# Slot input sums kept in SBUF, eight turning PSUM banks and other scheduler keys in an attention and soft-MoE kernel

## Chip, cores and metric

One core of a Trainium2 chip. The metric is the device time of one execution in microseconds (us). All times of instructions are from the profile of one execution and count from the start of its span. TensorE, VectorE, ScalarE, GpSimd and SyncE appear in the profile as PE (with PEld for weight loads), DVE, ACT, POOL and SP. The granted clock is the share of TensorE's full clock that the profile shows for a stretch. The record marks a run slow when it is over 1.5% above the fastest of its kernel; L834 is line 834 of that kernel's source. The changed kernel is nine lines longer, so that L834 of before is L843 after it.

## The reference

```
q, k, v: (8, 8, 576, 64) f32; phi: (512, 32); w1: (8, 512, 1024); w2: (8, 1024, 512)
scores = q k^T / 8 under a mask (heads 0-3: last 32 keys; heads 4-7: last 128, every 4th)
x      = softmax(scores) v, laid out as (4608, 512)
logits = x phi
d      = softmax of logits over the 4608 tokens;  slot_input = d^T x         (32 x 512)
slot_out[e] = relu(slot_input[e] w1[e]) w2[e]     for 8 experts of 4 slots
out    = softmax of logits over the 32 slots, times slot_out                 (4608 x 512)
```

## The kernel before

The program lists its operations with dependencies, an estimated cost each and a key. A list scheduler runs once, when the program is built: it walks through model time, picks for each engine, among the operations that can start soonest, the one with the lowest key, hands out PSUM banks, and so fixes each engine's order. Where TensorE would stand idle in model time, the scheduler may put in fillers, matmuls whose result nobody reads; they are meant to keep TensorE busy, so that its granted clock does not fall.

```
FILL = (125, 148)                 # model time, us, in which fillers may be put
...
# in schedule(): TensorE would stand idle from free["pe"] to t0, so fill the gap
if e == "pe" and fill[0] < t0 and free[e] < fill[1]:
    gap = t0 - max(free[e], fill[0])
    n = min(int((gap - 0.15) / 0.216), 64)      # matmuls of 128x512, 0.216 us each
    if gap > 0.4 and n > 0:
        x = filler(n)                            # matmuls whose result nobody reads
        ...
        place(x, ts, "pe")
...
ps  = A(nc.psum_tensor("ps", [128, 8, 512], F32))
psA = ps[:, 7, :]                                # bank 7: slot sums, held throughout
one = [[i] for i in range(7)]
psum = Pool(7, {1: [[6]] + one[:6], 2: [[0, 1], [2, 3], [4, 5]]})
...
PACE = 13.1                                      # key of work of unit u at offset x:
def due(u, x): return u * PACE + x               # due(u, x); 8 units of attention
...
# slot sums of batch b, all eight batches into one bank
i_ = t.matmul(psA[32*g:32*g+32, 256*ty:256*ty+256], sbt(et)[:, i, :],
              sbt((xb0, xb1)[ty])[:, m, :],
              start=b == 0 and i < 4, stop=b == B - 1, skip_group_check=True)
...
# after the last batch: one copy, then "fold" (f32 matmuls), w1, w2
op("dve", lambda vv: vv.tensor_copy(psA_sb[:], psA), r=[b_acc], w=[b_psA], ...)
...
PARTS = [("p3a",3,0,8), ("p0",0,0,16), ("p1",1,0,16), ("p2",2,0,16), ("p3b",3,8,16)]
# matmuls on the five parts of w2 in this order; the row sums stand after p1;
# p2 and p3b are loaded into TT, which attention has to leave first
```

The softmax here doesn't subtract the row's maximum and nothing guards it: scores larger than these inputs give would overflow.

## Time and profile before

| | before |
|---|---|
| time, median of 4 runs (of the later comparison) | 181.65 us (180.95 to 182.5) |
| fold matmuls begin (L768) | 137.9 us |
| row sums, then p2 and p3b (L849, L834) | 149.9, 151.9 us |
| last load (p3b) has landed | 151.8 us |
| slot outputs so_sb made (L860) | 153.24 us |
| end of span | 178.9 us |

The lines behind this table stand in the prediction. From so_sb on, 25.7 us of output follow, 22.4 us of them the output's own transfer.

In the list of waits, "issue" is time in which the engine waits for nothing that the profile shows (columns: total us, times, longest us).

```profile
PE ps L532 <- issue: 3.7, 4, 1.8
```

### The profile page before, as it was taken

To read this page: it belongs to the slowest core of one execution; us is meant where nothing else is said; L and a number is where in the kernel's file an instruction comes from. 1 tells how busy PE (TensorE), PEld (TensorE's weight loads), DVE (VectorE), ACT (ScalarE), POOL (GpSimd) and SP (SyncE) were. 2 spreads that over 40 slices of the span, in tenths; PEclk is the share of its full clock that TensorE was granted. 3 is DMA by queue.
4 is the path that set the end of the run, shared out by engine and by line. 5 is a ranking of instruction groups with operands and counts; after the bars stand their busy time and mean duration, and the time that the engine had idled before them with its cause. 6 is when DMAs were issued, how large, how long until landed. Compare 5 with 4: busy or idle time off the path is not lost.

```text
span 178.9 us, 5741 instructions
## 1 busy us (share of the span) xinstructions
PE 131.7 (74%) x2602; PEld 99.8 (56%) x2602; DVE 116.6 (65%) x262; ACT 92.1 (52%) x132; POOL 27.8 (16%) x56
## 2 busy tenths in 40 slices
PE   0019768885997977978898879788699999889000
PEld 0019557674775955756886757586565569432000
DVE  6980596994279569668859947969974020799200
ACT  2005957843574886568589557477331100599000
POOL 7960402500400250230020010010200000000000
PEclk9999999999699999999999999999999999999655
DMA  5999899999999999999999999999999993299995
GB/s 77 198 235 224 187 214 210 228 223 198 221 208 212 243 216 194 213 212 214 236 202 211 214 214 218 233 216 209 227 216 209 216 196 68 78 420 439 469 469 235
DMA packets 5015, 40.79 MB, mean 228 GB/s; under 512 B 1408, under 2 KB 1408, under 8 KB 1792
## 3 DMA queue, kind: packets, MB, share of 16 engines
q0 software_dynamic: 3600, 30.94, 82.9%
q1 hardware_dynamic: 1392, 9.50, 12.7%
q8 instruction: 20, 0.33, 0.7%
q14 instruction: 3, 0.02, 0.0%
HBM read 61.93 MB, written 9.44 MB: 399 GB/s over the span
## 4 chain that ended last, share of the span: by engine, by line
PE 44%; DVE 32%; ACT 6%; DMA 5%; issue 5%; POOL 1%; DVEq 0%; POOLq 0%
DVE XB L634 9%; DVE PT L584 9%; PE ps L532 7%; PE ps L678 5%; DVE WD L907 5%; DVE VN L599 5%; DMA stg<-in_v_dram 5%; PE ps L651 4%; PE ps L527 4%; PE ps L594 4%; PE ps L924 3%; ACT PT L576 3%; PE ps L569 3%; PE ps L623 2%; PE ps L787 2%
## 5 line engine op out<-in xcount | busy, mean ns | idle before, releaser
L551 ACT ACTIVATE TT<-ps 128x864 f32<-128x864 f32 x32 | 28.6, 896 | 32.9 <-PE ps L532 24.0
L576 ACT ACTIVATE PT<-ps 128x768 bf16<-128x768 f32 x48 | 36.7, 812 | 8.9 <-PE ps L569 8.8
L532 PE MATMUL ps<-ident,stg 96*64 96x96 bf16 x576 | 18.0, 224 | 18.3 <-DMA stg<-in_v_dram 12.8
L634 DVE TENSOR_TENSOR XB<-ps,RV 96x768 bf16<-96x768 f32 x32 | 30.3, 947 | 0.6
L532 PEld LDWEIGHTS ps<-ident,stg 96*64 96x64 bf16 x576 | 15.7, 123 | 20.0 <-DMA stg<-in_v_dram 12.8
L599 DVE COPY VN<-ps 128x768 bf16<-128x768 bf16 x32 | 17.5, 546 | 8.8 <-PE ps L594 8.6
L663 DVE COPY XT<-ps 128x576 bf16<-128x576 bf16 x19 | 11.4, 598 | 13.3 <-PE ps L651 13.2
L623 PE MATMUL ps<-VN,PT 128*128 128x65 bf16 x384 | 17.6, 194 | 1.9 <-DVE PT L584 0.9
L569 PE MATMUL ps<-TT 64*128 64x96 bf16 x384 | 15.1, 204 | 4.2 <-issue 1.1
L594 PE MATMUL ps<-ident,TT 128*128 128x128 bf16 x192 | 16.1, 221 | 1.6 <-issue 1.0
L623 PEld LDWEIGHTS ps<-VN,PT 128*128 128x128 bf16 x384 | 14.4, 98 | 4.0 <-DVE PT L584 1.3
L651 PE MATMUL ps<-ident,XB 96*128 96x96 bf16 x192 | 13.1, 209 | 4.4 <-DVE XB L634 4.3
L527 PE MATMUL ps<-ident,stg 96*128 96x96 bf16 x288 | 14.9, 206 | 0.1
L569 PEld LDWEIGHTS ps<-TT 64*128 64x128 bf16 x384 | 9.5, 94 | 7.9 <-ACT PT L576 1.4
L594 PEld LDWEIGHTS ps<-ident,TT 128*128 128x128 bf16 x192 | 10.9, 98 | 5.4 <-issue 2.4
L651 PEld LDWEIGHTS ps<-ident,XB 96*128 96x128 bf16 x192 | 9.8, 99 | 7.0 <-DVE XB L634 6.0
L584 DVE TENSOR_TENSOR PT<-PT,mask_d 128x768 bf16<-128x768 bf16 x24 | 12.9, 546 | 0.5 <-ACT PT L576 0.2
L527 PEld LDWEIGHTS ps<-ident,stg 96*128 96x128 bf16 x288 | 13.0, 98 | 0.3 <-ACT PT L576 0.3
L584 DVE TENSOR_TENSOR PT<-PT,mask_p 128x768 bf16<-128x768 bf16 x24 | 12.6, 538 | 0.0
L894 PE MATMUL ps<-so_sb,expT 128*128 128x512 bf16 x35 | 10.4, 397 | 0.7 <-DVE stg L907 0.2
L664 ACT ACTIVATE XT<-ps 128x576 bf16<-128x576 bf16 x13 | 8.4, 650 | 3.8 <-PE ps L651 3.5
L678 PE MATMUL ps<-XT,phi_pad 128*128 128x192 bf16 (+1 forms) x64 | 10.2, 306 | 0.2 <-ACT XT L664 0.2
(83 smaller groups left out, 162.6 us busy)
## 6 DMA issues: line engine op xcount, KB each, us to landing
WD<-in_moe_w_dram POOLq DMA_DIRECT2D x7, 1024.0 KB, 27.5
stg<-in_moe_w_dram POOLq DMA_DIRECT2D x2, 2048.0 KB, 19.1
out_dram<-WD SPq DMA_DIRECT2D x1, 4096.0 KB, 11.9
stg<-in_q_dram POOLq DMA_DIRECT2D x8, 288.0 KB, 14.9
stg<-in_k_dram POOLq DMA_DIRECT2D x8, 288.0 KB, 16.7
stg<-in_v_dram POOLq DMA_DIRECT2D x8, 288.0 KB, 18.7
stg<-in_q_dram POOLq DMA_DIRECT2D x4, 576.0 KB, 17.9
stg<-in_k_dram POOLq DMA_DIRECT2D x4, 576.0 KB, 19.8
```

What stands on the lines that cost most here:

```text
L527: i_ = t.transpose(bankb2(pt, a)[:, 96 * kk:96 * kk + 96], two[:, c, :], ident[0:96, 0:96])
L532: i_ = t.transpose(bankb2(pt, a)[64 * hx:64 * hx + 64, 96 * kk:96 * kk + 96], src[:, hx, c, :], ident[0:96, 0:96])
L551: return ac.activation(d, sv, ACTF.Copy)
L569: i_ = t.matmul(pair(sc)[:, hx, QB * x:QB * x + QB], win(u, 1, h01, blk_, bpar)[64 * hx:64 * hx + 64], win(u, 0, h01, blk_, bpar)[64 * hx: ...
L576: op("act", lambda ac: ac.activation(sbt(pt)[:, 0:768].rearrange("p (x n) -> p x n", x=2), pair(sc)[:, :, 0:384], ACTF.Exp, scale=SCALE), ...
L584: return dv.tensor_tensor(p_, p_, m.unsqueeze(1).to_broadcast([128, 2, 384]), AluOp.mult)
L594: i_ = t.transpose(bankb(pv)[:, 128 * m:128 * m + 128], win(u, 2, h01, m, bpar), ident[:, :])
L599: op("dve", lambda dv: dv.tensor_copy(sbt(vn)[:, :, :, 0:64], bankb(pv)[:, 0:768].rearrange("p (m x d) -> p m x d", m=6, x=2)), r=[pv], w= ...
L623: i_ = t.matmul(pair(po)[:, bk, 65 * po_:65 * po_ + 65], sbt(pts[i])[:, o_:o_ + 128], sbt(vn)[:, m, half, 0:65], start=True, stop=True)
L634: op("dve", lambda dv: dv.tensor_tensor(sbt(xb)[:].rearrange("p m (x h d) -> p h x m d", x=2, h=2)[:, h01], pv()[:, :, :, 0:64], sbt(rv)[: ...
L651: i_ = t.transpose(bankb(px)[:, QB * m:QB * m + QB], sbt(xb)[:, m, 128 * x:128 * x + 128], ident[0:QB, 0:QB])
L678: i_ = t.matmul(o_, phi_pad[:, c].rearrange("p j i -> p (j i)"), rhs, start=c == 0, stop=c == 3)
```

## The change

The intent is a shorter attention part: the slot sums of two batches at a time stay in a bank and are then added up in SBUF, so that all eight banks turn and pairs come from four places; other keys let the units overlap more; fillers start earlier, since attention should end earlier.

```
-FILL = (125, 148)
+FILL = (116, 148)
...
-    psA = ps[:, 7, :]
-    one = [[i] for i in range(7)]
-    psum = Pool(7, {1: [[6]] + one[:6], 2: [[0, 1], [2, 3], [4, 5]]})
+    psum = Pool(8, {1: [[i] for i in (6, 7, 0, 1, 2, 3, 4, 5)],
+                    2: [[0, 1], [2, 3], [4, 5], [6, 7]]})
...
-    PACE = 13.1
+    PACE = 10.87
...   (offsets of the stages changed: T 0.5 to 0.57 per step, S 4.0+1.3i to 5.2+1.13i,
       V 4.5 to 3.6, P 8.5+2.0g to 6.7+2.46g, X 13.0+0.8x to 19.2+0.1x, L 15.5 to 17.4)
-                i_ = t.matmul(psA[...], ..., start=b == 0 and i < 4, stop=b == B - 1, ...)
+                i_ = t.matmul(bank(acc)[...], ...,
+                              start=b % 2 == 0 and i < 4, stop=b % 2 == 1 and i % 6 >= 2, ...)
+        if b == 1:
+            op("dve", lambda dv: dv.tensor_copy(psA_sb[:], bank(acc)), ...)
+        elif b % 2:
+            op("dve", lambda dv: dv.tensor_tensor(psA_sb[:], bank(acc), psA_sb[:], AluOp.add), ...)
-    op("dve", lambda vv: vv.tensor_copy(psA_sb[:], psA), ...)        # once, at the end
```

(Also in the diff: a guard in the scheduler, so that nothing is picked that writes a bank not yet handed out, and two costs of the model, 0.22 to 0.28 us for S and 0.35 to 0.44 us for the slot sums.)

More of the change, by code (lines that the diff above doesn't have):

```diff
@@ L192, in schedule @@
                 got, tal, ok, taken = [], 0.0, True, {}
+                if any(t.phys is None and t not in o.alloc for t in o.touch):
+                    continue
                 for t in o.alloc:
@@ L341, in bass_dilated_sliding_attn__then__soft_moe_slots_kernel @@
     psb = ps[:].rearrange("p a x -> p (a x)").bitcast(BF16).rearrange("p (a x) -> p a x", a=8)
-    psA = ps[:, 7, :]
-    one = [[i] for i in range(7)]
-    psum = Pool(7, {1: [[6]] + one[:6], 2: [[0, 1], [2, 3], [4, 5]]})
+    psum = Pool(8, {1: [[i] for i in (6, 7, 0, 1, 2, 3, 4, 5)], 2: [[0, 1], [2, 3], [4, 5], [6, 7]]})
     def ring(ts):
@@ L378, in bass_dilated_sliding_attn__then__soft_moe_slots_kernel @@
     b_id0, b_id, b_sel, b_fold, b_rowm, b_phist, b_phi = [Buf() for _ in range(7)]
-    b_acc, b_psA, b_csum, b_rcs, b_rtok = [Buf() for _ in range(5)]
+    b_psA, b_csum, b_rcs, b_rtok = [Buf() for _ in range(4)]
     b_expT, b_expX = [Buf() for _ in range(B)], Buf()
@@ L503, in bass_dilated_sliding_attn__then__soft_moe_slots_kernel @@
     U = [dict() for _ in range(NU)]
-    XB, XT, ET = {}, {}, {}
+    XB, XT, ET, ACC = {}, {}, {}, {}
     def win(u, t, h01, i, bpar):
@@ L537, in st_T @@
            mode="h" if ty == 0 else "f",
-           key=due(u, 0.5 * j))
+           key=due(u, 0.57 * j))
         def ev(ac):
@@ L552, in st_T @@
         op("act", ev, r=[pt], **{"w" if j == 0 else "a": [b_TT[u % 2]]}, cost=0.8,
-           key=due(u, 0.8 + 0.5 * j))
+           key=due(u, 0.8 + 0.57 * j))
     def bankb2(t, a):
@@ L573, in pe @@
             return i_
-        k0 = due(u, 4.0 + 1.3 * i)
-        op("pe", pe, r=[b_TT[u % 2]], w=[sc], alloc=[sc, pt], cost=0.22, mode="r", key=k0)
+        k0 = due(u, 5.2 + 1.13 * i)
+        op("pe", pe, r=[b_TT[u % 2]], w=[sc], alloc=[sc, pt], cost=0.28, mode="r", key=k0)
         op("act", lambda ac: ac.activation(
@@ L596, in pe @@
             return i_
-        k0 = due(u, 4.5 + 2.0 * g)
+        k0 = due(u, 3.6 + 2.0 * g)
         op("pe", pe, r=[b_id, b_TT[u % 2]], w=[pv], alloc=[pv, vn], cost=0.35, key=k0)
@@ L626, in pe @@
             return i_
-        k0 = due(u, 8.5 + 2.0 * g)
+        k0 = due(u, 6.7 + 2.46 * g)
         op("pe", pe, r=list(pts.values()) + [vn], w=[po], alloc=al, cost=0.46, key=k0)
@@ L653, in pe @@
             return i_
-        k0 = due(u, 13.0 + 4.0 * bpar + 0.8 * x)
+        k0 = due(u, 19.2 + 4.0 * bpar + 0.1 * x)
         op("pe", pe, r=[b_id, xb], w=[px], alloc=al, cost=0.31, key=k0)
@@ L680, in pe @@
             return i_
-        k0 = due(u, 15.5 + 4.0 * (b % 2))
+        k0 = due(u, 17.4 + 4.0 * (b % 2))
         op("pe", pe, r=[x0, x1, b_phi], w=[lg], alloc=[lg], cost=1.0, key=k0)
@@ L716, in st_L @@
         xb0, xb1 = XB[b, 0], XB[b, 1]
+        if b % 2 == 0:
+            ACC[b // 2] = tile(psum, 1)
+        acc = ACC[b // 2]
         def pe3(t):
@@ L721, in pe3 @@
                 g = (m + 2 * ty) % 4
-                i_ = t.matmul(psA[32 * g:32 * g + 32, 256 * ty:256 * ty + 256],
+                i_ = t.matmul(bank(acc)[32 * g:32 * g + 32, 256 * ty:256 * ty + 256],
                               sbt(et)[:, i, :], sbt((xb0, xb1)[ty])[:, m, :],
-                              start=b == 0 and i < 4, stop=b == B - 1,
+                              start=b % 2 == 0 and i < 4, stop=b % 2 == 1 and i % 6 >= 2,
                               skip_group_check=True)
             return i_
-        op("pe", pe3, r=[et, xb0, xb1], a=[b_acc], cost=0.35, mode="c", key=k0 + 4.0)
+        op("pe", pe3, r=[et, xb0, xb1], after=list(acc.ready), a=[acc],
+           alloc=[acc] if b % 2 == 0 else [], cost=0.44, mode="c", key=k0 + 4.0)
+        if b == 1:
+            op("dve", lambda dv: dv.tensor_copy(psA_sb[:], bank(acc)), r=[acc], w=[b_psA],
+               cost=0.6, key=k0 + 4.6)
+        elif b % 2:
+            op("dve", lambda dv: dv.tensor_tensor(psA_sb[:], bank(acc), psA_sb[:], AluOp.add),
+               r=[acc], w=[b_psA], cost=0.6, key=k0 + 4.6)
     W_AFTER = {2: ["w10"], 3: ["w11"], 4: ["w12"], 5: ["w13"], 6: ["w14"],
@@ L762, in bass_dilated_sliding_attn__then__soft_moe_slots_kernel @@
     op("dve", lambda vv: vv.reciprocal(rcs[:], rcs[:]), w=[b_rcs], cost=0.1, key=K1)
-    op("dve", lambda vv: vv.tensor_copy(psA_sb[:], psA), r=[b_acc], w=[b_psA], cost=0.65, key=K1)
     fo = tile(psum, 1)
```

## The prediction

> **What bounds the kernel now.** I read, in this order, the page's rows and queue table, its chain, a table of windows over the last 60 us, the last loads with the timeline of what uses them, and the waits.
>
> ```profile
> span 178.9 us, 5741 instructions
> ...
> PE 131.7 (74%) x2602; PEld 99.8 (56%) x2602; DVE 116.6 (65%) x262; ACT 92.1 (52%) x132; POOL 27.8 (16%) x56
> ...
> DMA  5999899999999999999999999999999993299995
> ...
> q0 software_dynamic: 3600, 30.94, 82.9%
> ...
> q8 instruction: 20, 0.33, 0.7%
> ...
> PE 44%; DVE 32%; ACT 6%; DMA 5%; issue 5%; POOL 1%; DVEq 0%; POOLq 0%
> ```
>
> The last line, the chain that ended last, calls the kernel bound by compute: 44% TensorE, 32% VectorE, 5% DMA. The change is made with that in view. The DMA row says something else: the 16 engines are busy in nearly every slice until about 147 us, fall to 3 and 2 tenths for two slices, and are then filled by the output. The queue table sizes that wall. The loads' packets (q0) take 82.9% of 16 engines' span: 0.829 x 178.9 = 148.3 us on each engine. Instruction fetches add 0.7%, 1.3 us. The bytes begin to flow at about 2.4 us. So 2.4 + 148.3 + 1.3 = 152.0 us is when the loads end, as long as their number, size and rate stay as they are. The windows show whether anything interrupts them (columns: window and length in us; busy us of PE, PEld, DVE, ACT, POOL with counts; granted clock; DMA share; GB/s).
>
> ```profile
> 118.00:128.00 10.00, 7.33 (x158) 5.71 (x154) 8.54 (x19) 6.55 (x9) 1.58 (x3) 1.00 1.03 221
> 128.00:138.00 10.00, 9.72 (x117) 5.79 (x117) 6.71 (x17) 2.78 (x6) 0.00 (x0) 1.00 1.02 218
> 138.00:148.00 10.00, 10.00 (x130) 6.36 (x133) 1.41 (x3) 0.98 (x2) 0.00 (x0) 1.00 0.95 200
> 148.00:154.00 6.00, 5.62 (x162) 4.96 (x151) 0.87 (x2) 0.47 (x1) 0.00 (x0) 1.00 0.20 41
> 154.00:166.00 12.00, 10.55 (x37) 3.66 (x36) 11.90 (x19) 11.20 (x18) 0.00 (x0) 1.00 0.88 363
> ```
>
> Nothing does: the share is 1.0 up to 138 and 0.95 up to 148, and the windows from 4 to 138 us all move 207 to 221 GB/s (counted as landed bf16). Then: who is late at the end, compute or loads? Two issue rows give the time to landing of the last two parts of the second weight matrix, p2 and p3b; the timeline shows their issue and their use.
>
> ```profile
> TT<-in_moe_w_dram POOLq DMA_DIRECT2D x1, 2048.0 KB, 20.0
> ...
> TT<-in_moe_w_dram POOLq DMA_DIRECT2D x1, 1024.0 KB, 25.1
> ...
> 126.16 1.05 POOL L430 DMA_DIRECT2D TT<-in_moe_w_dram  x2 [5.87 <-PE ps L569]
> ...
> 149.94 2.04 PE L849 MATMUL ps<-rowm,expT 128*128 128x1 bf16 x36
> 151.91 1.21 PEld L834 LDWEIGHTS ps<-TT,hT 128*32 128x32 bf16 x48
> 151.91 1.49 PE L834 MATMUL ps<-TT,hT 128*32 128x256 bf16 x48
> 152.02 0.38 DVE L854 RECIPROCAL rtok<-ps 128x36 f32<-128x36 f32 x1 [4.59 <-PE ps L849]
> 153.24 0.48 DVE L860 TENSOR_SCALAR so_sb<-ps,rcs 128x256 bf16<-128x256 f32 x1 [0.84 <-PE ps L834]
> ```
>
> p2 lands at 126.2 + 20.0 = 146.2 us. p3b, issued half a microsecond after it, lands at 126.7 + 25.1 = 151.8 us, which agrees with the 152.0 above. TensorE comes to these parts at 151.91, after its row sums (L849), and then runs all 48 matmuls: 32 on p2, which has lain there for 5.7 us, and 16 on p3b, which has just come. So compute and loads finish within 0.1 us of each other: two bounds, of which the chain shows one.
>
> [...] The loads read f32 and land bf16, so 214 GB/s landed is 428 GB/s read[...]. [...] Here GpSimd waits for a free buffer before each load, but each load takes 15 to 25 us from issue to landing, so the queue stays full meanwhile. [...] after TensorE stood still from 42.3 to 44.1 us its clock was 0.50 to 0.66 until 48 us. Pauses of 1.1 us (near 77 and 103 us) left it at 1.00. [...] Before, one holds the slot sums throughout, and a pair can take three places.
>
> **The change part by part.**
> Slot sums: the accumulation over eight batches becomes four over two. The matmuls stay the same in number; only their start and stop flags differ. VectorE empties the bank four times in place of once. The one copy of 128x512 f32 took 0.69 us (L763); I take 0.7 us for each add as well. That is 3 x 0.7 = 2.1 us more on VectorE (116.6 to 118.7), spread over some 100 us; only the last stands on the tail, where the copy stood: 0 to 0.1 us.
> Banks: eight singles and four pair places for seven and three. What this can take away is in the waits of TensorE for an engine that empties a bank:
>
> ```profile
> PE ps L532 <- ACT TT L551: 1.0, 2, 0.5
> PE ps L569 <- DVE VN L599: 1.0, 1, 1.0
> PE ps L569 <- ACT PT L576: 0.9, 1, 0.9
> ```
>
> With the smaller ones about 4 us over the whole attention part. Since the order was fixed for seven banks, part of the cost lies in the order itself, so I allow 3 to 8 us in all.
> Keys: a pace of 10.87 for 13.1 and other offsets let a unit start further inside the one before. No instruction is added. The filler matmuls' start moves from 125 to 116, as if the attention's end was expected 9 us earlier. I choose 5 us, for VectorE is already busy 11.2 of 15 us per unit and TensorE 12.5. The fold matmuls (L768), at 137.9 us before, then begin at about 133, and everything up to p1 is done before p2 lands.
> Tail: p2's 32 matmuls can run when it lands at 146.2, and the row sums are done by then too. At 151.8 only p3b's 16 are left. 48 took 1.49 us, of which the last one's latency is 0.27; the step is (1.49 - 0.27) / 47 = 0.026 us. 32 fewer are 0.83 us; the start itself moves from 151.91 to about 151.85. **Sum**: 0.83 + 0.06 = 0.9 us. The output starts 0.9 us earlier and is as long as before, since it is its own DMA wall (363 to 391 GB/s to the end). Of a 5 us gain in compute some 4 us turn into waiting for p3b. If TensorE's clock has fallen by then, the 16 matmuls and the first ones of the output cost about 0.4 us more; at even odds that is 0.2. So 0.7 us off: 181.75 - 0.7 = 181.05, which I round to 181.0, with a profiled span of about 178.2.
>
> **The rivals.**
> A: compute is the only bound, as the chain reads. Then 5 us fewer in attention give 176.8, and the full 9 us give 172.8. Against it stands p3b's landing at 151.8; for it, only if the last loads finish late because they are issued late. The queue speaks against that: p1 was issued at 119.8, p2 at 126.2, and p1 was landing until about 138, so p2 waited in the queue for 10 us and more.
> B: waiting takes the place of compute and lets the clock fall. The fillers end by the scheduler's 148, so TensorE may stand idle for 2 to 4 us before p3b. At half clock the tail loses what the shorter queue won: 181.5 to 182.
> C: VectorE becomes the bound. It carries 2.1 us more, and the new order may make TensorE wait for it. For it: VectorE is 32% of the chain. Even then compute must become slower than before to cost anything, since it now ends level with the loads: 182.5 to 184.
> D: the loads' end itself moves. The last of the 16 engines ends about 4 us after the first (share 0.95, then 0.20, with data until 151), and 20 instruction fetches fall unevenly among them. More fillers mean more instructions. This shifts the end by up to 1 us either way.
>
> **Range and chances.** The DMA wall gives 181.0. The three runs before spread over 181.0 to 182.5, and D gives 1 us either way: 180.0 to 182.2 should hold it 8 times in 10. Faster by over 2% needs 178.1 or less, 3.6 us off, which the loads forbid unless A is right: 0.05. Slower by over 2% needs 185.4, which C alone hardly reaches: 0.02. Within 2%: 0.93.
>
> **What would show it.** Right: the DMA row and the windows' GB/s unchanged up to 147 us; p3b landing at 151 to 152.5; L768 well before 137.9; L834 on TT split in two, 32 soon after 146 and 16 at the end, the latter released by the DMA and with idle time before them; the first so_sb row (L860) at about 152.4 in place of 153.24; four evictions of the slot sums at about 0.7 us each; a chain that now names the load of TT. Wrong: L834 still running without a pause after compute that ends late (C), or the loads landing several us earlier with the share at 1.0 (then the wall was not one, A). A clock under 1.00 around 152 us would show B.

## The result and the profile after

The changed kernel takes 192.75 us (188.91 to 194.32, 4 runs), against 181.65 us. Its fast runs are 1.047 times those of before (95% interval 1.033 to 1.061). All ratios here are the mean time of one kernel's fast runs over that of the other's of the same rounds, so they are not quite the ratios of the medians. Two of the four runs (194.03 and 194.32) are marked slow and are not used in the ratio; medians and ranges are of all runs. The profiled run is a fast one, 191.48 us.

The page of the changed kernel, the lines that answer to those of before:

```profile
span 189.3 us, 5828 instructions
...
DMA  5999999999999999999999999999999300399992
...
q0 software_dynamic: 3600, 30.94, 78.2%
...
q8 instruction: 21, 0.34, 0.7%
...
PE 55%; DVE 14%; ACT 10%; issue 8%; DMA 5%; POOL 1%; DVEq 0%; POOLq 0%
```

The loads are as they were (0.782 x 189.3 = 148.0 us on each engine) and the DMA row is full as long as before. But two slices after it are empty: but for one fetch of instructions, the engines stand still from 151 us until the output begins at 164 us. The page's issue row for p3b and its issue tell that the last load is not what is late: it is issued at 121.5 and lands at 121.5 + 29.7 = 151.2 us.

```profile
TT<-in_moe_w_dram POOLq DMA_DIRECT2D x1, 1024.0 KB, 29.7
...
120.94 1.05 POOL L430 DMA_DIRECT2D TT<-in_moe_w_dram  x2 [4.99 <-PE ps L569]
```

The timeline shows what TensorE does from then on (start, length, engine, line, operation, count):

```profile
149.37 2.04 PE L858 MATMUL ps<-rowm,expT 128*128 128x1 bf16 x36
...
151.48 7.07 PE L933 MATMUL ps<-mask_p,ident 128*128 128x512 bf16 x32
...
158.48 1.06 PE L843 MATMUL ps<-TT,hT 128*32 128x256 bf16 x32
...
159.69 1.67 PE L933 MATMUL ps<-mask_p,ident 128*128 128x512 bf16 x7 [0.16 <-issue]
...
161.30 0.62 PE L843 MATMUL ps<-TT,hT 128*32 128x256 bf16 x16
161.75 0.48 DVE L869 TENSOR_SCALAR so_sb<-ps,rcs 128x256 bf16<-128x256 f32 x1 [9.93 <-PE ps L843]
```

L933 is the filler. 33 fillers stand between the row sums and p2, and 8 between p2 and p3b (the trace lacks two of the records). All data is there at 151.2 us; TensorE then spends 41 x 0.216 = 8.9 us on matmuls that nobody reads. From the first of them to so_sb it is 10.54 us, against 1.33 us from the same point before; so_sb comes 8.51 us later, since that point itself is 0.70 us earlier.

The output is longer too: from so_sb to the end of the span 27.55 us, against 25.66. The packets show where: fifteen of the 16 DMA engines are done at about 186.5 us and one goes on alone until 188.4 (share 0.06). The sum is 8.51 + 1.89 = 10.4 us, the whole difference of the spans.

And attention gained little: the fold begins at 136.7 in place of 137.9 us, 1.2 us, where I had chosen 5. The list of waits of the changed kernel says where the rest is: the same line as before, now with more than twice the time.

```profile
PE ps L532 <- issue: 8.2, 4, 4.3
```

**Where these stalls lie.** I numbered TensorE's records in the trace (weight loads, matmuls and the few waits that stand by themselves) in order of start. Every "issue" stall of more than 0.6 us in the attention part begins at record 193 + 256k (or the next one or two), in both kernels, and some 1.2 to 1.7 us before it ends one instruction fetch of 16 KB (the packets of queue q8) has come in. Some blocks of 256 records, times in us:

```
kernel  record  its block before  its fetch        stall   fetch end
                began                                      to restart
before  1217    37.37             41.54 to 42.63   1.82    1.50
before  1985    58.90             62.75 to 63.72   1.17    1.36
before  3521    97.69             101.48 to 102.65 1.08    1.40
after   1217    34.98             40.09 to 41.03   4.30    1.52
after   2241    64.51             68.30 to 69.19   2.30    1.57
after   3521    95.97             99.91 to 100.88  1.53    1.38
after   5313    150.91            151.25 to 152.17 none    -
```

While the loads keep the DMA engines full (share 0.95 to 1.07 in windows of 6 to 12 us before), the fetch of a block starts some 2 to 5 us after the block before it has begun, mostly 3.7; it takes about 0.95 us, and TensorE goes on 1.2 to 1.7 us after its end. With the usual lag, 256 records so take some 3.7 + 0.95 + 1.4 = 6.1 us (an estimate; the shortest block of a run took 4.8 to 5.9 us). Where TensorE's work is denser, it stalls. The pauses over 0.3 us that begin at a record 193 + 256k add up to 5.7 us before and 12.6 us after. That the fetch is the cause was only read from the trace at this point; the experiments e5 and e6 test it.

The scheduler knows no such stalls. Its own schedule put the fold at 134.9 us before and at 124.1 us after. On the chip it came 3.0 us later than that before, and 12.6 us later after. Fillers for a gap from 138.0 to 145.1 of model time thus ran from 151 to 158 us.

My theory was then: (1) the loads and compute end almost level, as predicted; (2) the late fillers are the loss of 8.5 us; (3) instruction fetches eat most of attention's gain (the granted clock turned out to have a part in this, see e3 and e4), and a 21st fetch that falls into the output costs the other 1.9 us. Rivals: the new order or the added evictions cost the time; or TensorE's clock does.

### The profile page after: what moved, and what is told of

It is laid out like the page before. It is cut to its first block, busy times and chain, and to the rows that moved or that the text cites.

```text
span 189.3 us, 5828 instructions
## 1 busy us (share of the span) xinstructions
PE 141.2 (75%) x2635; PEld 106.6 (56%) x2642; DVE 110.8 (59%) x253; ACT 97.8 (52%) x144; POOL 27.8 (15%) x56
## 4 chain that ended last, share of the span: by engine, by line
PE 55%; DVE 14%; ACT 10%; issue 8%; DMA 5%; POOL 1%; DVEq 0%; POOLq 0%
PE ps L532 10%; PE ps L933 7%; PE ps L527 7%; ACT PT L576 6%; PE ps L623 6%; PE ps L678 5%; DVE WD L916 5%; DMA stg<-in_v_dram 5%; PE ps L594 3%; PE ps L569 3%; PE ps L651 3%; DVE XB L634 2%; PE ps L843 2%; DVE PT L584 2%; PE ps L796 2%
## 5 line engine op out<-in xcount | busy, mean ns | idle before, releaser
L532 PE MATMUL ps<-ident,stg 96*64 96x96 bf16 x576 | 18.3, 234 | 21.0 <-DMA stg<-in_v_dram 12.5
L532 PEld LDWEIGHTS ps<-ident,stg 96*64 96x64 bf16 x576 | 16.9, 131 | 21.9 <-DMA stg<-in_v_dram 12.5
L664 ACT ACTIVATE XT<-ps 128x576 bf16<-128x576 bf16 x25 | 15.7, 656 | 6.7 <-PE ps L651 6.7
L594 PE MATMUL ps<-ident,TT 128*128 128x128 bf16 x192 | 17.0, 226 | 1.1 <-ACT TT L551 1.0
L569 PE MATMUL ps<-TT 64*128 64x96 bf16 x384 | 16.3, 207 | 2.0 <-issue 1.4
L632 DVE RECIPROCAL RV<-ps 96x12 f32<-96x12 f32 x32 | 7.0, 221 | 16.7 <-PE ps L623 16.4
L933 PE MATMUL ps<-mask_p,ident 128*128 128x512 bf16 x59 | 14.5, 382 | 0.8 <-issue 0.7
L594 PEld LDWEIGHTS ps<-ident,TT 128*128 128x128 bf16 x192 | 11.6, 102 | 3.6 <-ACT TT L551 1.5
L584 DVE TENSOR_TENSOR PT<-PT,mask_d 128x768 bf16<-128x768 bf16 x24 | 12.3, 527 | 0.0
L678 PE MATMUL ps<-XT,phi_pad 128*128 128x192 bf16 (+1 forms) x64 | 11.0, 323 | 1.0 <-ACT XT L664 1.0
L651 PEld LDWEIGHTS ps<-ident,XB 96*128 96x128 bf16 x192 | 10.5, 104 | 1.1 <-DVE XB L634 0.4
```

The costliest lines, as they stand in the source:

```text
L532: i_ = t.transpose(bankb2(pt, a)[64 * hx:64 * hx + 64, 96 * kk:96 * kk + 96], src[:, hx, c, :], ident[0:96, 0:96])
L569: i_ = t.matmul(pair(sc)[:, hx, QB * x:QB * x + QB], win(u, 1, h01, blk_, bpar)[64 * hx:64 * hx + 64], win(u, 0, h01, blk_, bpar)[64 * hx: ...
L584: return dv.tensor_tensor(p_, p_, m.unsqueeze(1).to_broadcast([128, 2, 384]), AluOp.mult)
L594: i_ = t.transpose(bankb(pv)[:, 128 * m:128 * m + 128], win(u, 2, h01, m, bpar), ident[:, :])
L651: i_ = t.transpose(bankb(px)[:, QB * m:QB * m + QB], sbt(xb)[:, m, 128 * x:128 * x + 128], ident[0:QB, 0:QB])
L678: i_ = t.matmul(o_, phi_pad[:, c].rearrange("p j i -> p (j i)"), rhs, start=c == 0, stop=c == 3)
```

## The experiments

A table of what the traces show first; "schedule" is where the program's own schedule puts the fold, "stalls" the sum of pauses described above. The times of instructions are of one profiled run each; e5 and e6 ran once, so their state is unknown. Each run is explained below the table; e7 and e9, whose profiled runs were slow, are left out of it.

| run | edit | schedule | fold begins | stalls | so_sb | so_sb to end | time, median us |
|---|---|---|---|---|---|---|---|
| before | | 134.9 | 137.9 | 5.7 | 153.2 | 25.7 | 181.65 |
| after | | 124.1 | 136.7 | 12.6 | 161.75 | 27.55 | 192.75 |
| e1 | after, no late fillers | 124.1 | 135.9 | 11.0 | 152.1 | 25.6 | 180.64 |
| e2 | before, 41 late fillers | 134.9 | 137.2 | 3.9 | 161.6 | 25.6 | 191.98 |
| e3 | banks alone | 131.0 | 135.7 | 6.9 | 152.2 | 25.7 | 180.09 |
| e4 | keys alone | 127.9 | 135.5 | 6.8 | 152.15 | 26.45 | 181.04 |
| e5 | e1, five loads moved back | 124.1 | 134.0 | 7.3 | 163.55 | 26.35 | 192.11 |
| e6 | e1, 128 instructions in front | 124.1 | 136.4 | 10.2 | 152.5 | 27.4 | 182.19 |
| e8 | e3, one load more | 131.05 | 140.8 | 8.5 | 156.8 | 26.0 | 184.60 |
| e10 | e3 again | 131.0 | 139.4 | 7.3 | 154.75 | 25.65 | 183.37 |
| e11 | e3, fillers from 112 | 131.0 | 136.8 | 7.8 | 152.1 | 25.6 | 180.28 |
| e12 | e1, fillers from 106 | 124.1 | 132.5 | 9.6 | 152.15 | 26.55 | 180.66 |

### e1: the changed kernel without late fillers

```
-FILL = (116, 148)
+FILL = (116, 137)
```

> The changed kernel with the window for filler matmuls ended at 137 in place of 148, so that the 33 fillers between the row sums and part p2 of the second weight matrix, and the 8 between p2 and p3b, fall away; nothing else differs. Theory (the late fillers, placed for an attention part that was expected to end at 124 and ends at 136.7, hold TensorE past the landing of the loads): the matmuls on p2 and p3b follow the row sums at about 151.3, so_sb is made at about 152.6 in place of 161.8, the span is 178 to 179 us and the time 180.5 to 182. With 82 TensorE instructions fewer the last instruction fetch no longer falls into the output. Rival 1 (the new order or the extra evictions themselves cost the time): it stays above 186. Rival 2 (TensorE's clock falls without the late fillers): so_sb comes at 152.6 but the clock near 152 is under 1.00 and the time is 182 to 184.

Measured: 180.64 us (179.93 to 180.87), ratio to before 0.997 (0.992 to 1.002). so_sb at 152.08. The loss is gone with one number, and nothing else of the change was touched: the schedule of e1 is that of the changed kernel without the 33 and the 8 fillers. Both rivals fall: neither the order nor the evictions cost time, and the clock did not fall near 152 us: the 48 matmuls on p2 and p3b took 1.71 us with the 0.31 us of waiting for p3b in it, against 1.49 us before at a clock of 1.00. The timeline of e1:

```profile
150.54 1.71 PE L843 MATMUL ps<-TT,hT 128*32 128x256 bf16 x48
151.63 0.34 PEld L843 LDWEIGHTS ps<-TT,hT 128*32 128x32 bf16 x16 [0.31 <-DMA TT<-in_moe_w_dram]
152.08 0.48 DVE L869 TENSOR_SCALAR so_sb<-ps,rcs 128x256 bf16<-128x256 f32 x1 [1.05 <-PE ps L843]
```

The second row is the one the prediction had asked for: 16 weight loads on p3b, released by the DMA of TT after an idle 0.31 us.

### e2: the kernel before with late fillers

```
+        if k_ >= 3:                       # k_ 3: part p2, k_ 4: part p3b
+            late = [op("pe", lf, ..., after=[last_], cost=0.216 * n, ...)]   # n = 33, 8
...
-    last_ = op("pe", pe, ...)
+    last_ = op("pe", pe, ..., after=late)
```

> The kernel before with one thing added: 33 filler matmuls between the row sums and part p2, and 8 between p2 and p3b, as the changed kernel has them. Theory (late fillers): so_sb comes 33 x 0.216 + 8 x 0.216 = 8.9 us later, the time is 189.5 to 193, like the changed kernel. As the TensorE stream passes the same block of 256 instructions at its end, the output should also end 1 to 2 us later than the shift alone. Rival 1 (order or evictions): it stays at 181 to 183, for the fillers would run in time that TensorE waits anyway.

Measured: 191.98 us (189.45 to 193.92; the runs over 193 are marked slow), ratio 1.050 (1.041 to 1.059), about the change's 1.047. so_sb at 161.60. So the same fillers in the old order cost the same. The output did not become longer in the profiled run (25.6 us): the 21st fetch came, but only at 188.4 us, after the output. That part of what I expected missed.

### e3 and e4: the two parts by themselves

e3 takes the change and puts back the old pace, offsets and the old S cost; `FILL = (125, 144)`. e4 takes the kernel before and puts in the new ones; `FILL = (116, 141)`. Neither has late fillers.

> Only the banks part of the change (slot sums in SBUF, eight banks, pairs from four places), with the keys of the kernel before, and the filler window ended at 144 so that no late fillers come. The program's own schedule puts the fold matmuls at 131.0, 3.9 us earlier than before (134.9). Theory (stalls of TensorE at blocks of 256 instructions eat a gain in attention, and the loads set the end): the fold begins at 134 to 138, the time is 180.5 to 182. Rival (the banks help as the schedule says and compute is the bound): the fold begins at 134 and the time falls to 178. Rival (extra evictions on VectorE cost): the fold begins later than 138 and the time is above 183.

Measured: 180.09 us (179.84 to 180.11), ratio 0.994 (0.989 to 1.000). Fold at 135.7, stalls 6.9 us; the time is just under the range that I gave.

> Only the keys part of the change (the pace and the offsets), with seven banks and one accumulator as before, and the filler window 116 to 141 so that no late fillers come. The program's own schedule puts the fold matmuls at 127.9, 7.0 us earlier than before. Theory (stalls at blocks of 256 instructions, loads set the end): the keys pack TensorE's work more densely, so the summed stalls grow from 5.7 us to 9 to 13, the fold begins at 134 to 138, and the time is 180.5 to 182. Rival (compute is the bound): fold near 131, time near 175. Rival (the keys make VectorE the bound): no growth of the stalls, fold later than 138, time above 182.

Measured: 181.04 us (180.88 to 181.18), ratio 1.000 (0.995 to 1.005). Fold at 135.5, in the range; stalls 6.8 us, where I had expected 9 to 13: a miss. In these single traces each part alone has the fold some 2.3 us earlier, and both together (e1) no more: 2.0 us; but e10, which is e3's kernel again, has it 1.5 us later than before, so a gain of this size is within what varies from run to run. The schedules differ by 10.8 us from before to after, the chip's folds by 2.4 at most in these.

Stalls alone do not say how late the fold is against its schedule: e3 and e4 have the same stalls (6.9 and 6.8 us) but are 4.7 and 7.6 us late. What differs is the clock: counted from TensorE's first matmul (12.8 us) to the fold, it was below full for 11 us in e3 and for 22 us in e4. (The time before the first record of the full clock, at 17.0 us before and 18.1 after, counts as below full: the transposes of 96x96 took 281 ns there, as at a clock of 0.50 near 45 us, and 206 ns at 1.00, all in the trace of before.) Over the twelve profiled runs that are not marked slow, lateness is about the stalls (factor 1.0) plus 0.29 us for each us below the full clock, less 5.5 us, to within 0.9 us; this is a fit, not an experiment. By it the 9.6 us that the changed kernel is later than before are some 7 us of stalls (5.7 to 12.6) and some 3 us of clock (8 us to 19 us below full). In e4 TensorE waited for the last load; its mean granted clock was 0.903 (e3: 0.950), and from so_sb to the end it took 26.45 us, close to the 26.55 of e12, where the clock was 0.50 when the load came.

### e5: loads moved, so that the DMA engines pause

```
+    late = [o for o in P.order if o in early_w]          # loads of w10 to w14
+    P.order = [o for o in P.order if o not in early_w]
+    at = P.order.index(last_unit) + 1                    # behind the last unit's load
+    P.order[at:at] = late
```

> As the first run (changed kernel, no late fillers), with the loads of five of the first weight matrices (w10 to w14) moved behind the load of the last attention unit, so that the 16 DMA engines have pauses during the first half of attention; TensorE's order is the same, instruction by instruction. The result stays right; the loads end later, so the time is worse on purpose. Theory (TensorE's stalls come from instruction fetches that queue behind the loads): in the first eight blocks of 256 instructions the fetch starts sooner after its block (lag under 1 us where the engines pause, against 2.5 to 5.1), the stalls up to 76 us fall from 7.7 us to under 3, and the same matmul that began at 70.8 us begins at 63 to 67. Rival (the stalls are waits for other engines or bubbles of TensorE itself): stalls of 4.3 and 2.3 us stay at the same instructions.

Measured: 192.11 us, late on purpose. The windows of e1 and of e5 (in this order) from 58 to 72 us, with DMA share and GB/s at the end of the row:

```profile
58.00:72.00 14.00, 11.54 (x319) 9.58 (x320) 10.71 (x22) 9.96 (x15) 4.11 (x9) 1.00 1.02 216
```

```profile
58.00:72.00 14.00, 12.99 (x347) 11.02 (x345) 11.44 (x24) 11.03 (x17) 2.97 (x6) 1.00 0.70 130
```

With the engines at 0.70, TensorE does more in the same 14 us. Over the six blocks that begin at records 1473 to 2753 the mean lag of the fetch falls from 3.6 us (e1) to 1.7 us, with 0.46 us as the least, and the stalls from 3.5 to 0.7 us. Up to record 1217 the engines were still full (share 0.97 from 30 to 44 us), and the stall there stayed: 3.2 us against 2.9. So the number that I had set for all stalls up to 76 us (under 3 us) was missed, with 4.7 us against 6.9, and record 2241 began no earlier (70.4 against 68.9), because e5 had been 3 us behind already at 32 us. The trace shows why: in e5 the record of the full clock begins only at 26.4 us (e1: 16.7), and from 17 to 25.5 us its transposes of 96x96 (L535; L532 in e1) took 281 ns on average in place of 206; at record 449 it is 2.9 us behind. So the lag and the stalls fall where the engines pause; the total that I had expected was not reached.

### e6: 128 instructions in front

```
+    def pe_sh(t):
+        for _ in range(64):
+            i_ = t.matmul(bank(sh)[:, 0:32], ident[:, :], ident[:, 0:32], ...)
+    op("pe", pe_sh, r=[b_id], w=[sh], alloc=[sh], cost=2.0, key=-5)
```

> As the first run (changed kernel, no late fillers), with 64 small matmuls, that is 128 TensorE instructions, put in front while TensorE waits for the first load. Theory (stalls come where a block of 256 instructions ends): the stalls stay at instructions 193 + 256k counted from the start, so they move by 128 against the work; the 4.3 us stall at work instruction 1217 is gone or small and others stand at 1089 and 1345 of the work. The end of attention may move by 2 us either way, the time stays at 180.5 to 182 since the loads set it. Rival (stalls belong to the work, through a wait on another engine): they stay at the same matmuls, index 1217 + 128 from the start.

Measured: 182.19 us, one run, just above the range that I gave. The stalls over 0.6 us begin at records 1217, 1473, 2241, 2497, 3521 and 3777 from the start, that is at 1089, 1345, 2113, 2369, 3393 and 3649 of the work. The stall at work record 1217 (2.9 us in e1) is gone. A wait on another engine would have stayed with its matmul; these stalls stay with the count. (The size of a single stall varies between runs of one order: at record 3521 it was 3.0 us in e1 and 1.5 in the changed kernel. Their places do not.) With its 5378 records the stream passes record 5313, its 21st fetch comes at 162.6 us in the middle of the output, and the output takes 27.4 us. Again one DMA engine ends alone, 1.8 us after the other fifteen (177.2 and 179.0 us). That is the changed kernel's 27.55 (5331 records, fetch at 176.7); e1 and e3, with 5256 and 5246 records, have 20 fetches and 25.6 and 25.7 us.

### e7: no fillers at all

```
-FILL = (116, 148)
+FILL = (1000, 1000)
```

> The changed kernel with no fillers at all. Theory (late fillers are the whole loss): so_sb at 152 to 153.5, time 181 to 183. If fillers are worth their place by the clock, the granted clock falls to 0.5 somewhere between 125 and 155 us and the feed-forward part takes 1 to 3 us longer, which the loads hide in part: up to 183.5. Rival (order or evictions cost the time): above 186.

Measured: 187.53 us (slow, the profiled one) and 182.60 us. In the profiled run the clock was at 0.50 from 128 to 149 us and the fold came at 140.5. I take no size from one slow and one fast run. The fast one is above all of e1's (180.87 at most), which fits that fillers before the fold and between the feed-forward stages have a use; that is not shown.

### e8 and e9: one load more, one load less

e8 reads the first expert's first weights a second time into the same place. e9 leaves out the second expert's and uses the first one's, so its result is wrong. Both start from e3.

> The banks part alone (third run), with one load more: the first expert's first weights are read a second time into the same place, 1024 KB landed, 2 MB read, in the middle of attention. The result stays right. Theory (the loads' queue is never empty and sets the end once compute is in time): everything behind it lands 1.05 MB / 0.214 MB per us = 4.9 us later, p3b at 156 to 157, so_sb at about 157, the time 184.5 to 186. Rival (compute is the bound, loads have room): p3b later, but the time within 1 us of the third run's 180.1.

Measured: 184.60 us (two runs, 184.56 and 184.63), correct. p3b lands at 156.3, TensorE waits 0.41 us for it, so_sb at 156.8:

```profile
156.33 0.62 PE L851 MATMUL ps<-TT,hT 128*32 128x256 bf16 x16 [0.41 <-DMA TT<-in_moe_w_dram]
```

One load of 4.9 us costs 4.5 us against e3's 180.09 (another chip), and 3.9 us against the kernel before in the same rounds (1.021, 1.016 to 1.027): the loads are a bound and their queue has no room. Compute was late too in this run (fold at 140.8).

> The banks part alone, with one load less: the second expert uses the first expert's first weights, so the result is wrong on purpose. Theory (two bounds that end almost level): p3b lands 4.9 us earlier, near 147, but the row sums end at about 149.7 as in the third run, and then all 48 matmuls follow; so_sb at about 151 in place of 152.2, the time 178.5 to 179.8, a gain of only about 1 us. Rival (only the loads bound): the full 4.9 us, time near 175.

Measured: 183.74 us (slow, the profiled one) and 178.98 us. p3b lands at 146.7, 5 us earlier; but in the profiled run the clock was lower (0.916 on average, against 0.944 in the fast run) and the fold began at 140.6, so so_sb came at 156.0. The one fast run is in the range that I gave. This agrees with two bounds that end nearly level, but one fast run does not show it.

### e10: e3 once more, five rounds

> The banks part alone once more, against the kernel before in five rounds, as the version that may beat both. Theory: its so_sb comes 1.0 us earlier than before (152.2 against 153.2), so the time is 0.4 to 0.8% lower, 180 to 180.6, and the interval excludes 1. Rival (the gain is noise): ratio within 0.998 to 1.002.

Measured: 183.37 us (180.22 to 184.85), ratio of the fast runs 1.002 (0.995 to 1.009). So e3's gain was not confirmed; three of the six runs are marked slow. The traces of two fast runs of this kernel show a difference in the clock: windows of e3 and then of e10, the granted clock is the third number from the right.

```profile
122.00:126.00 4.00, 1.79 (x36) 1.40 (x36) 4.00 (x9) 0.65 (x1) 0.00 (x0) 1.00 1.00 213
126.00:130.00 4.00, 3.06 (x20) 2.15 (x21) 2.00 (x5) 1.39 (x3) 0.00 (x0) 0.57 0.96 205
130.00:134.00 4.00, 3.96 (x50) 2.56 (x50) 1.38 (x6) 0.74 (x2) 0.00 (x0) 1.00 1.02 217
```

```profile
126.00:130.00 4.00, 2.84 (x21) 2.07 (x21) 3.02 (x6) 0.65 (x1) 0.00 (x0) 0.52 0.98 209
130.00:134.00 4.00, 3.26 (x22) 2.19 (x21) 0.99 (x3) 1.39 (x3) 0.00 (x0) 0.50 0.98 209
```

VectorE is busy throughout from 122 to 126 us and TensorE waits for it, busy 1.79 of 4 us. Then the clock of TensorE is at half (0.52 from 126 to 128 us in e3, 0.50 from 128 to 136 us in e10): for one stretch of 3.4 us in e3, for three in e10, where it was also at half from 99 to 106 us. There the fold comes 3.7 us later and compute falls behind the loads.

### e11 and e12: fillers earlier, none late

```
e11, from e3:        -FILL = (125, 144)      e12, from e1:        -FILL = (116, 137)
                     +FILL = (112, 144)                           +FILL = (106, 137)
```

> The banks part alone, with the filler window opened at 112 in place of 125, which adds some 13 fillers in the last 8 us before the last sums, where TensorE was half idle and its granted clock fell to 0.50 for one stretch in the third run and for three in the tenth. Theory (the spread of 180 to 185 us between runs of the banks part is that fall of the clock, which pushes compute behind the loads): the clock between 118 and 138 us is 1.00 or falls for one stretch at most, the fold begins at 134.5 to 136.5, all runs lie at 179.8 to 181.0, and the ratio to the kernel before is 0.992 to 0.998. Rival (the fillers delay real work and nothing is won): fold later than 136.5, time 181 to 183.

Measured: 180.28 us (179.86 to 180.53), ratio 0.997 (0.995 to 1.000). All six runs lie within 0.7 us, where e10 spread over 4.6, and the clock is 1.00 from 110 to 142 us. The fold, at 136.8, was later than I had put it, for the clock had fallen earlier in that run (0.50 from 98 to 108). It is the steadiest version: faster than both kernels, against before by 0.3%, which is less than matters.

> The changed kernel with the filler window 106 to 137: no late fillers, as in the first run, and some 10 more before the last sums. Theory: the clock falls less there, fold at 134.5 to 136.5, time 179.8 to 181.0 in all runs, ratio 0.992 to 0.998. Rival: as the first run or worse, 180.5 to 183.

Measured: 180.66 us (179.81 to 185.08), ratio 0.997 (0.994 to 1.001). Not all runs stayed under 181 (185.08 is marked slow). Its trace is the best test of the prediction's main claim. The fold begins at 132.5 (earlier than I had put it), which is 5.4 us earlier than before and 4.2 earlier than in e11, and so_sb comes at 152.15, as in e11:

```profile
147.20 1.67 PE L843 MATMUL ps<-TT,hT 128*32 128x256 bf16 x32
...
151.49 1.04 PE L843 MATMUL ps<-TT,hT 128*32 128x256 bf16 x16 [2.61 <-DMA TT<-in_moe_w_dram]
152.15 0.48 DVE L869 TENSOR_SCALAR so_sb<-ps,rcs 128x256 bf16<-128x256 f32 x1 [4.46 <-PE ps L843]
```

TensorE comes to p2's matmuls 3.6 us earlier than in e11 (147.20 and 150.78). Of this, 2.61 us turned into waiting for the load and the rest went to the clock, which was at half when the load came (0.50 from 148 to 158 us): the 16 matmuls take 1.04 in place of 0.62 us, and so_sb to the end takes 26.55 in place of 25.6 us.

## Why the prediction was wrong

The prediction was 181.0 us (180.0 to 182.2) with 0.93 for "within 2%"; measured 192.75 us, slower by 4.7%.

- **The loads' wall: right.** p3b landed at 151.2 (predicted 151 to 152.5), 0.6 us earlier than before, though it was issued 5.2 us earlier. One reading was off, without effect: the loads took not 15 to 25 us from issue to landing but up to 27.5 (the page's median for seven of the first weight matrices). e8 puts the wall 4.9 us later and the time follows by 3.9 to 4.5; e12 brings compute 5.4 us forward and so_sb by 1.1. Rival A (compute alone bounds) falls.
- **The failed step** is in the part on the tail: "p2's 32 matmuls can run when it lands at 146.2, and the row sums are done by then too. At 151.8 only p3b's 16 are left." In their place stood 33 and 8 fillers in TensorE's order, 8.9 us, and p2's matmuls began at 158.5 us. The diff showed the filler window, and I used it only to guess how much earlier attention should end. In rival B I wrote that the fillers end "by the scheduler's 148" and read 148 as a time on the chip. But the window is only the rule by which a count of fillers is chosen when the program is built. The count holds for the gap in the model, 138.0 to 145.1 us; on the chip there was no gap left. e1 (fillers out: 180.64 us) and e2 (the same fillers in the old kernel: 191.98 us) show that this step is nearly the whole loss. Without it the sum holds: so_sb at 152.08, predicted 152.4; e1 took 180.64 us, predicted 181.0. It holds with little to spare: TensorE came to p2's matmuls at 150.5, not soon after 146, and waited 0.31 us for p3b where the prediction had some 4 us.
- **The size of attention's gain was off**: 5 us chosen, 1.2 measured (2.0 in e1). The row "issue" was there before, 5% of the chain, and I did not ask what it was. It is instruction fetch behind the loads: the stalls grew from 5.7 to 12.6 us, and beside them the time below the full clock before the fold from 8 to 19 us (see e4). This alone would have cost nothing, since e1 still ends with the loads. Together with fillers cut for a fold at 124 us it made the loss.
- **The output**: I took it to be as long as before. It was 1.9 us longer. With 41 late fillers the stream passed record 5313 and a 21st fetch fell into the output; e6, which passes it by other instructions, shows the same 1.8 us, and in both one DMA engine ends that much after the rest. In rival D I had fillers bringing more fetches, but only for the loads' end.
- **Rival C** (VectorE): the add of the sums took 0.68 us, about as estimated, and e3 lost nothing by it. VectorE's busy time did not grow by 2.1 us; it fell from 116.6 to 110.8 us, because the scheduler may put the copies into XT (L663, L664) on either engine and now put 25 of 32 on ScalarE, where 13 had been. It rightly had little weight.
- **Rival B** (the clock): it did not make the loss, but it is real and about as large as the gain. In e12 it took 0.42 us of the 16 matmuls and 0.95 us of the output; I had put 0.4 on both.

Open: why the changed kernel and e2 spread over 5 us from run to run (e1 and e11: under 1 us). A 21st fetch at a varying place in the output, or fillers at half clock, would fit; neither was tested.

## What to carry to other kernels

A filler or any other work whose amount is fixed when the program is built is as good as the model of time behind it; put it where a late predecessor cannot push needed work, and count it again in the trace after every change of the schedule. Before working out what a faster stage is worth, look at what ends level with it, here a load queue that kept the DMA engines busy (share 0.95 to 1.07) from 4 to 148 us. And where "issue" time grows with density, number the engine's instructions: here the stalls returned at record 193 + 256k, and stayed there when e6 put 128 instructions in front of the work, so they belonged to the instruction stream and not to the data.

## What the traces showed of fetches, output and clock

- Instruction fetch: 20 or 21 fetches of 16 KB per run (20 before, 21 after), stalls at 193 + 256k. Beside a full queue of loads the pauses there were 3.9 us (e2) to 12.6 us (changed kernel) in all per run of the table: the next block's fetch began mostly 3.7 us after the block before it (2 to 5; 0.3 us before and after where the loads had ended), took 0.95 us, and TensorE went on 1.2 to 1.7 us later. That is about 6.1 us per 256 records, the estimate worked out above from these three.
- A fetch in the middle of an output transfer: the output's packets took 24.1 and 24.2 us with it (e6, changed kernel), 22.4 to 23.0 us in the other twelve traces.
- TensorE's clock: it fell to half (0.52) after 4 us in which TensorE was busy for 1.79 us (e3, 122 to 126 us). In the kernel before it was 0.50 to 0.66 after TensorE had stood still for 1.8 us (42.3 to 44.1 us) and stayed at 1.00 over pauses of 1.1 us; in e3 it stayed at 1.00 from 98 to 102 us, though TensorE was busy for 0.10 us in the first 2 us of them. So no single length of pause was shown at which it falls.
- DMA: the loads read 2 x 214 = 428 GB/s for 145 us, while slices of the output showed 439 to 469 GB/s (page of the kernel before).
